# Attention and a two-layer MLP in one kernel: three split products of the second layer in the slots that close a pair, and the second batch's first and last pair summed on VectorE

## The chip, the core and the metric

The kernel runs on one core of one Trainium2 chip. A core has five engines that run side by side and wait for each other through semaphores: TensorE (PE) multiplies matrices, with its weight loads (PEld) shown apart; VectorE (DVE) and ScalarE (ACT) work on elements; GpSimd (POOL) does slower elementwise work and issues some of the DMAs; SyncE (SP) issues the other DMAs. TensorE writes to PSUM, which is divided into banks; everything else lies in SBUF. The metric is device time in microseconds (us), the median of several runs.

## The reference

The inputs are q, k and v of shape 8 x 12 x 448 x 64 (batch, heads, sequence, head size), two gains of 64 numbers, and two matrices of weights, 768 x 2048 and 2048 x 768. All are f32. What is computed, cut to what matters:

```
q_n = q / sqrt(mean(q*q, -1) + 1e-6) * g_q          # the same for k with g_k
scores = q_n @ k_n.T / 8                             # per batch and head, 448 x 448
attn = exp(scores - max) ; attn = attn / (attn.sum(-1) + 1e-9)
x = (attn @ v), heads side by side                   # 3584 x 768
h = x @ w_in ;  g = 0.5*h*(1 + tanh(0.79788*(h + 0.044715*h**3)))
out = g @ w_out                                      # 3584 x 768
```

## The kernel before

**Stages.** The batches b = 0 to 7 are taken in turn. For each there is an attention stage and a stage of the first MLP layer. The second MLP layer of one batch is spread into the attention stage of the next, so that TensorE has work while ScalarE computes exps. So from b = 1 on, `attention(b, ...)` mixes the attention of batch b with a quota of second-layer products of the batches before: 96 for b = 1 and 112 for the others. After it, `mm1(b, f)` computes the first layer of batch b in 16 groups of six matmuls, ended by a GELU on ScalarE. The change's title counts from one: its "batch 2" is b = 1 in the code and in this text.

**Pairs and slots.** The 12 heads of a batch are six pairs, hp = 0 to 5. The keys of a head are cut into four tiles of 112. `scores` (line 198) makes the scores of one key tile for both heads of a pair, two matmuls of 64 rows that run at the same time, into one of two PSUM buffers, and an exp on ScalarE turns them into the bf16 tile `ex`. `attention` (line 359) goes through a pair in two slots. In the even slot it issues the scores of key tiles 0 and 1; in the odd slot those of tiles 2 and 3. An even slot from the second pair on also ends the pair before it (`pair_ends`, line 260): the products of `ex` with v (called x here) into one PSUM tile, and the sums over keys, as products with a matrix of ones, into another. Both write 64 columns per head, so that the two heads' matmuls run at the same time.

**Second-layer products.** They are a list, taken from the front by `upto` (line 365). One output tile takes 16 of them; then VectorE copies the tile to SBUF (line 317), and SP sends out the row when both halves are there. The tiles share two PSUM buffers with the first layer's. In the first pair's two slots 20 and 10 products are issued; after that `even` products in each even slot, ahead of `pair_ends`, each cut into two halves of 64 columns (`parts` = 2), and whole ones in each odd slot, so many that the quota less 30 and less `last` is used up in equal steps. `last` holds how many come before and after the last pair's `pair_ends`.

**Sums over keys.** For b of 2 and more, `key_sums` (line 212) adds the exps of key tiles 0 and 1, and of 2 and 3, on VectorE (line 220); for the first and the last pair it also adds the two results (line 222). The sums then take two steps of two matmuls in the middle pairs, and one step in the first and last pair, in place of four. For b = 1 all pairs take four steps, directly from the exps.

**What VectorE does for a pair.** `pair_recips` transposes the sums (line 244), takes reciprocals (line 245) and transposes back (line 246); `pair_x` multiplies x by them (line 251). VectorE works through its instructions in the order in which they are written out, and the copies of output tiles, the adds of `key_sums`, the gains of the keys (`gain`, line 191, in `side`) and the sums of squares (line 127) stand in the same queue.

**Order.** `manual_schedule` keeps each engine's instructions in the order of the code. `side` and `m1` are plans that say in which slot or first-layer group a preparing step of a later batch is issued. In `m1`, at group 0, GpSimd starts the norms of the next batch (`normed_all`); for b of 2 and more a one-element copy (`gpsimd_waits`, line 527) stands ahead of them that waits for the last pair's added exps. SP issues the transposing DMAs of these norms at groups 4, 8 and 12.

Of the kernel before, what the change touches and what calls it, by code (L numbers as in the profile page):

```python
# [16 lines left out]
def kernel(  # L17
# [19 lines left out]
    HP = H // 2  # L37
# [86 lines left out]
    def total(b, c, n, hs=slice(0, CH)):  # L124
        if b not in sss:
            sss[b] = smp.tile([P, NCH, 2, CH, NK], F32, tag="ss", name="ss")
        nc.vector.reduce_sum(  # L127
            sss[b][:, c, "qk".index(n), hs], sqs[n, b, c][:, hs], axis=AX.X
        )
# [11 lines left out]
    def idle(n, w):  # L141

        for _ in range(n):
            nc.tensor.matmul(w, zeros[:, :128], zeros, start=True, stop=True)
# [51 lines left out]
    exs, ess, oas = {}, {}, {}  # L196

    def scores(b, hp, kt):
        if kt == 0:
            exs[b, hp] = exq.tile([P, NK, 2, S], BF16, tag="ex", name="ex")  # L200
        sc = ps_s.tile([128, 2, 512], F32, tag="sc", name="sc")
        for a in range(2):
            r = slice(a * D, (a + 1) * D)
            nc.tensor.matmul(  # L204
                sc[:, a, :S], kT[r, hp, kt], qT[b][r, hp],
                start=True, stop=True,
            )
        nc.scalar.activation(  # L208
            exs[b, hp][:, kt], sc[:P, :, :S], AF.Exp, scale=scale, bias=shift
        )  # L210

    def key_sums(b, hp, i):


        if b < 2:
            return
        if i == 0:
            ess[b, hp] = exq.tile([P, 2, 2, S], BF16, tag="es", name="es")
        ex, es = exs[b, hp], ess[b, hp]
        nc.vector.tensor_add(es[:, i], ex[:, 2 * i], ex[:, 2 * i + 1])  # L220
        if i == 1 and hp in (0, HP - 1):
            nc.vector.tensor_add(es[:, 0], es[:, 0], es[:, 1])  # L222

    def pair_products(b, hp, what, waits=0):


        o = oas[what] = ps_o.tile([128, S], F32, tag=f"o{what}", name=f"o{what}")
        idle(waits, o)

        e = exs[b, hp] if what or b < 2 else ess[b, hp]  # L230
        n = 1 if not what and b > 1 and hp in (0, HP - 1) else e.shape[1]
        for i in range(n):
            for a in range(2):
                nc.tensor.matmul(  # L234
                    o[a * D:(a + 1) * D], vb[b % 2][:, 2 * hp + a, i] if what else ones, e[:, i, a],
                    start=(i == 0), stop=(i == n - 1),
                )

    def pair_recips():

        st = stp.tile([128, S // 32, 32], F32, tag="st", name="st")
        oas["rb"] = stp.tile([128, S], F32, tag="rb", name="rb")
        rc = smp.tile([128, S // 32], F32, tag="rc", name="rc")
        nc.vector.transpose(st.rearrange("p a b -> p (a b)"), oas[0])  # L244
        nc.vector.reciprocal(rc, st[:, :, 0])
        nc.vector.transpose(oas["rb"], rc.to_broadcast([128, S // 32, 32]))  # L246

    def pair_x(b, hp):
        if hp == 0:
            xT[b] = xp.tile([128, HP, S], BF16, tag="xT", name="xT")  # L250
        nc.vector.tensor_mul(xT[b][:, hp], oas[1], oas["rb"])  # L251
# [7 lines left out]

    def pair_ends(b, hp):  # L260

        for what in (1, 0) if b > 1 else (0, 1):
            pair_products(b, hp, what)
        pair_recips()
        pair_x(b, hp)
# [93 lines left out]
    def attention(b, m2, quota, side):  # L359


        first, last, even = (20, 30), (12, 12) if b > 1 else (17, 7), 2 if b > 1 else 0
        given = 0

        def upto(k, parts=1):
            nonlocal given
            while given < k:
                m2.pop(0)(parts)
                given += 1

        spread = quota - first[1] - sum(last)
        for hp in range(HP):
            for odd in range(2):
                i = 2 * hp + odd
                for fn in side.get(i, ()):
                    fn()
                if hp and not odd:
                    key_sums(b, hp - 1, 1)
                for kt in range(2 * odd, 2 * odd + 2):
                    scores(b, hp, kt)  # L380
                if not hp:
                    upto(first[odd])
                elif odd:
                    upto(first[1] + spread * hp // (HP - 1))
                else:

                    upto(given + even, 2)
                    pair_ends(b, hp - 1)
                if not odd:
                    key_sums(b, hp, 0)  # L390
        key_sums(b, HP - 1, 1)
        nc.scalar.preload_act_table_set(GELU_SET)
        upto(given + last[0])
        pair_ends(b, HP - 1)
        upto(quota)

# [130 lines left out]
    def gpsimd_waits(x):  # L527

        nc.gpsimd.tensor_copy(mark, x)  # L529
# [44 lines left out]
    for b in range(B):  # L574
        m1, side = [], []
        if b == 0:

            m1 = [(1, lambda: total(1, 0, "k"), lambda: total(1, 1, "q"),
                   lambda: total(1, 1, "k"), lambda: total(1, 2, "k"), lambda: total(1, 2, "q"),
                   lambda: nc.scalar.preload_act_table_set(EXP_SET), lambda: rsqrt(1),  # L580
                   lambda: nc.scalar.preload_act_table_set(GELU_SET),  # L581
                   lambda: load_v(1, CH, 2 * CH), lambda: normed1(0), lambda: normed1(1)),
                  (3, lambda: loads(2, 0)),
                  (4, lambda: trans(1, 0, ps_m), lambda: normed1(2), lambda: transposed(1, 1),
                   lambda: loads(2, 1)),
                  (5, lambda: trans(1, 1, ps_m), lambda: loads(2, 2),
                   lambda: pool_waits(1, 2, "k", 1), lambda: square(2, 0, "q", nc.gpsimd),
                   lambda: square(2, 0, "k", nc.gpsimd)),
                  (6, lambda: trans(1, 4, ps_m)), (7, lambda: trans(1, 5, ps_m))]
            side += [(0, lambda: total(2, 0, "q"), lambda: total(2, 0, "k")),  # L590
                     (2, lambda: gain(1, 1))]

            for c, slots in ((1, (5, 7)), (2, (9, 10))):
                for n, slot in zip("qk", slots):
                    side += [(2 * c - 1, lambda c=c, n=n: square(2, c, n, nc.gpsimd)),
                             (slot, lambda c=c, n=n: total(2, c, n))]
        elif b + 1 < B:
            if b > 1:

                m1.append((0, lambda: gpsimd_waits(ess[b, HP - 1][:1, 0, 0, :1])))  # L600
            for c in range(NCH):
                m1 += [(0, lambda c=c: normed_all(b + 1, c)),
                       (4 * c + 4, lambda c=c: transposed(b + 1, c))]
            m1 += [(9, lambda: gain(b + 1, 0)), (14, lambda: gain(b + 1, 1))]
            side.append((3, lambda: gain(b + 1, 2)))
        if 0 < b and b + 2 < B:
            m1 += [(4, lambda: loads(b + 2, 1)), (8, lambda: loads(b + 2, 2))]
            for c, at in ((0, 1), (1, 9)):
                for i, (n, half) in enumerate((n, half) for n in "qk" for half in range(2)):
                    m1.append((at + i, lambda c=c, n=n, half=half: squared(b + 2, c, n, half)))  # L610
                m1 += [(at + 2, lambda c=c: total(b + 2, c, "q")),
                       (at + 4, lambda c=c: total(b + 2, c, "k"))]
            for n in "qk":
                m1.append((13, lambda n=n: square(b + 2, 2, n, nc.gpsimd)))
                side.append((0, lambda n=n: total(b + 2, 2, n)))
        m1 = plan(*m1)
        for f in range(nf // 2 if b == 0 else nf):
            if b > 0:
                mm1(b, f)
            elif f > 1:  # L620
                mm1_pair(f)
            for fn in m1.get(f, ()):
                fn()
        m2 += m2_parts(b)
        if b + 1 == B:
            for fn in m2:
                fn()
            break
        nc.scalar.preload_act_table_set(EXP_SET)
        if b + 2 < B:  # L630
            side += [(11, lambda: rsqrt(b + 2)),
                     (0 if b else 2, lambda: load_v(b + 2, 0, H))]
            if b + 3 < B:
                side.append((1, lambda: loads(b + 3, 0)))
        attention(b + 1, m2, 96 if b == 0 else 112, plan(*side))


# [28 lines left out]
```

## Time and profile before

| | us |
|---|---|
| median of 3 runs (lowest, highest) | 442.35 (442.12, 442.97) |
| the profiled execution's own time | 442.38 |
| its span, first to last instruction | 440.6 |
| attention stage of b = 1 with 96 products (59.60 to 92.06) | 32.46 |
| attention stage of b = 2 with 112 products (110.32 to 142.98) | 32.66 |
| attention stages of b = 3 to 7, each | 32.66 |
| TensorE busy in the stage of b = 2 | 32.54 |
| ScalarE / VectorE busy in the stage of b = 2 | 26.38 / 25.36 |
| first layer of one batch, 96 matmuls | 18.16 |

The granted TensorE clock is 0.999 of full speed over the span. The profile's busy shares count a matmul from its start to its modelled end, so a TensorE that is busy all the time may still wait. What it waits for is seen in the starts of single instructions: a matmul of 448 columns follows its neighbour after 0.19 us when nothing holds it, one of 384 columns after 0.16 us. In lines of the timeline the first number is the start, the second the time from the first start to the last end of a run of equal instructions, and the bracket at the end tells how long the engine was idle before it and what released it.

### The profile page before, as it was taken

Reading aid. Unit: us, or ns where it says so; the run is one execution under the profiler, and the core shown is the slowest. Engines: PE = TensorE matmul, PEld = TensorE weight load, DVE = VectorE, ACT = ScalarE, POOL = GpSimd, SP = SyncE. Lnnn points to the kernel's source line nnn. Section 1 sums busy time; section 2 is a strip of 40 time slices with the busy share of each in tenths; the row PEclk is TensorE's granted clock in tenths of the full one; section 3 lists DMA queues with packets and bytes.
Section 4 is the critical chain, followed back from the end, with each engine's and each line's share of the span. In section 5 each row is a group of like instructions: output and inputs, shape, how many; then the busy total and the mean of one; then the engine's idle time right before and its main releaser. Section 6 shows DMA issues by size and latency. Waiting matters only on the chain.

```text
span 440.6 us, 7132 instructions
## 1 busy us (share of the span) xinstructions
PE 428.7 (97%) x2827; PEld 215.2 (49%) x2827; DVE 258.9 (59%) x446; ACT 306.2 (69%) x407; POOL 149.9 (34%) x138
## 2 busy tenths in 40 slices
PE   8898999999999999999999999999999999999996
PEld 3344554455445554455445544455544554455563
DVE  5889846834688357763688536872588603881010
ACT  5896568946886688857888578856889348863310
POOL 5998126482202940065400950037400730000000
PEclk9999999999999999999999999999999999999999
DMA  8999999569801868139911779119831431111022
GB/s 202 241 233 238 211 190 259 80 152 250 169 18 55 190 111 176 36 93 224 194 37 36 170 159 182 37 37 230 128 70 36 99 65 37 38 36 37 0 72 72
DMA packets 79218, 54.02 MB, mean 123 GB/s; under 512 B 37456, under 2 KB 74192, under 8 KB 79184
## 3 DMA queue, kind: packets, MB, share of 16 engines
q1 hardware_dynamic: 62240, 41.66, 40.5%
q0 software_dynamic: 16624, 11.80, 18.2%
q8 instruction: 22, 0.36, 0.3%
q10 hardware_dynamic: 320, 0.10, 0.1%
q14 instruction: 12, 0.10, 0.1%
HBM read 45.61 MB, written 11.01 MB: 129 GB/s over the span
## 4 chain that ended last, share of the span: by engine, by line
PE 87%; ACT 8%; DMA 3%; DVE 1%; issue 0%; SPq 0%; POOL 0%; ACTq 0%; DVEq 0%
PE o L293 34%; PE h L272 29%; PE o L234 11%; PE sc L204 10%; ACT ex L208 6%; PE hh L339 3%; DMA vb<-in_v_dram 2%; DMA rawq<-in_q_dram 1%; ACT g L344 1%; PE tp L166 0%; SPq L95 0%; ACT L581 0%; ACT L580 0%; POOL g L122 0%; DVE st L244 0%
## 5 line engine op out<-in xcount | busy, mean ns | idle before, releaser
L208 ACT ACTIVATE ex<-sc,shift 112x896 bf16<-112x896 f32 x192 | 182.4, 1003 | 21.6 <-PE sc L204 21.2
L293 PE MATMUL o<-wout,g 128*128 128x384 bf16 (+1 forms) x956 | 161.2, 328 | 0.0
L272 PE MATMUL h<-xT,win 128*128 128x448 bf16 x672 | 128.3, 352 | 0.0
L293 PEld LDWEIGHTS <-g 128*128 128x128 bf16 (+1 forms) x956 | 81.4, 99 | 70.3 <-issue 23.4
L276 ACT ACTIVATE g<-h 128x448 bf16<-128x448 f32 x112 | 61.0, 544 | 75.2 <-PE h L272 72.3
L272 PEld LDWEIGHTS <-win 128*128 128x128 bf16 x672 | 65.8, 98 | 61.0
L127 DVE TENSOR_REDUCE ss<-sq 112x16 f32<-112x1024 f32 (+1 forms) x44 | 50.1, 1143 | 62.1 <-ACT sq L120 58.9
L204 PE MATMUL sc<-qT,kT 64*128 64x448 bf16 x384 | 58.8, 355 | 4.9 <-ACT ex L208 2.7
L317 DVE COPY osb<-o 128x384 f32<-128x384 f32 x51 | 28.1, 551 | 50.9 <-PE o L293 50.0
L220 DVE TENSOR_TENSOR es<-ex 112x896 bf16<-112x896 bf16 x72 | 43.9, 617 | 10.2 <-ACT ex L208 10.0
L529 POOL COPY mark<-es 1x1 bf16<-1x1 bf16 x5 | 0.9, 178 | 140.0 <-DVE es L222 140.0
L244 DVE STREAM_TRANSPOSE st<-o 128x448 f32<-128x448 f32 x48 | 31.2, 649 | 26.7 <-PE o L234 26.0
L234 PE MATMUL o<-ex,vb 112*64 112x448 bf16 x384 | 44.7, 354 | 0.6 <-DMA vb<-in_v_dram 0.6
L149 POOL TENSOR_TENSOR nrmk<-rawk,rinv 112x512 bf16<-112x512 f32 x40 | 44.5, 1130 | 0.0
L149 POOL TENSOR_TENSOR nrmq<-rawq,rinv 112x512 bf16<-112x512 f32 x40 | 41.0, 1043 | 4.8 <-ACT rinv L139 4.8
L204 PEld LDWEIGHTS <-kT 64*128 64x128 bf16 x384 | 17.2, 93 | 46.4 <-issue 41.2
L251 DVE TENSOR_TENSOR xT<-o,rb 128x448 bf16<-128x448 f32 x48 | 30.0, 625 | 3.8 <-PE o L234 1.7
L246 DVE STREAM_TRANSPOSE rb<-rc 128x448 f32<-128x448 f32 x48 | 31.0, 645 | 1.6
L122 POOL TENSOR_TENSOR sq<-rawq 112x1024 f32<-112x1024 f32 x9 | 17.1, 1894 | 40.1 <-DMA rawq<-in_q_dram 26.0
L234 PEld LDWEIGHTS <-vb 112*64 112x64 bf16 x384 | 20.9, 109 | 14.7 <-issue 2.3
L122 POOL TENSOR_TENSOR sq<-rawk 112x1024 f32<-112x1024 f32 (+1 forms) x11 | 19.5, 1774 | 4.9 <-DVE ss L127 3.3
L339 PE MATMUL hh<-xT,win 128*128 128x448 bf16 x96 | 19.1, 352 | 1.4 <-ACT g L344 0.8
(60 smaller groups left out, 235.9 us busy)
## 6 DMA issues: line engine op xcount, KB each, us to landing
rawq<-in_q_dram SPq DMA_DIRECT2D x22, 448.0 KB, 5.4
rawk<-in_k_dram SPq DMA_DIRECT2D x22, 448.0 KB, 6.5
vb<-in_v_dram POOLq DMA_DIRECT2D x6, 672.0 KB, 7.4
win<-in_moe_w_in_dram POOLq DMA_DIRECT2D x2, 1536.0 KB, 18.5
wout<-in_moe_w_out_dram POOLq DMA_DIRECT2D x2, 1536.0 KB, 21.6
out_dram<-osb SPq DMA_DIRECT2D x7, 336.0 KB, 2.7
out_dram<-osb SPq DMA_DIRECT2D x8, 288.0 KB, 2.7
out_dram<-osb SPq DMA_DIRECT2D x8, 240.0 KB, 2.7
```

The lines of the kernel that those rows point to most:

```text
L122: eng.tensor_mul(sq, raw, raw)
L127: nc.vector.reduce_sum(sss[b][:, c, "qk".index(n), hs], sqs[n, b, c][:, hs], axis=AX.X)
L149: eng.tensor_mul(nrms[n, b, c][:, j].rearrange("p t a d -> p a t d"), raws[n, b, c][:, 2 * j:2 * j + 2], rinvs[b][:, c, "qk".index(n), 2 * ...
L204: nc.tensor.matmul(sc[:, a, :S], kT[r, hp, kt], qT[b][r, hp], start=True, stop=True,)
L208: nc.scalar.activation(exs[b, hp][:, kt], sc[:P, :, :S], AF.Exp, scale=scale, bias=shift)
L220: nc.vector.tensor_add(es[:, i], ex[:, 2 * i], ex[:, 2 * i + 1])
L234: nc.tensor.matmul(o[a * D:(a + 1) * D], vb[b % 2][:, 2 * hp + a, i] if what else ones, e[:, i, a], start=(i == 0), stop=(i == n - 1),)
L244: nc.vector.transpose(st.rearrange("p a b -> p (a b)"), oas[0])
L272: nc.tensor.matmul(h[:, :S], win[:, c, f * 128:(f + 1) * 128], xT[b][:, c], start=(c == 0), stop=(c == HP - 1),)
L276: nc.scalar.activation(g[:, f, (b % 2) * S:(b % 2 + 1) * S], h[:, :S], AF.Gelu_apprx_tanh)
L293: nc.tensor.matmul(o[j * m:(j + 1) * m, :HD], g[:, f, i * 128 + j * m:i * 128 + (j + 1) * m], wout[:, f, half * HD:(half + 1) * HD], start ...
L339: nc.tensor.matmul(h[:, j, :S], win[:, c, f * 128:(f + 1) * 128], xT[0][:, c], start=(c == 0), stop=(c == HP - 1),)
```

## The change

- In `attention`, `even` becomes 3 instead of 2 for b of 2 and more. It stays 0 for b = 1. The quota stays, so each odd slot issues one whole product fewer.
- For b = 1, `last` becomes (12, 12) instead of (17, 7), as for the later batches.
- `key_sums` adds exps for the first and last pair of b = 1 too: three adds each on VectorE. The sums of these two pairs then take one step instead of four.
- In `pair_ends` of b = 1, x's products come ahead of the sums for all pairs, as for the later batches.
- In b = 1's first-layer stage GpSimd too waits for the last pair's added exps before the next batch's norms.

```diff
     def key_sums(b, hp, i):
-        if b < 2:
+        if b < 1 or b == 1 and 0 < hp < HP - 1:
             return
...
     def pair_products(b, hp, what, waits=0):
...
-        e = exs[b, hp] if what or b < 2 else ess[b, hp]
-        n = 1 if not what and b > 1 and hp in (0, HP - 1) else e.shape[1]
+        e = exs[b, hp] if what or (b, hp) not in ess else ess[b, hp]
+        n = 1 if not what and b and hp in (0, HP - 1) else e.shape[1]
...
     def pair_ends(b, hp):
-        for what in (1, 0) if b > 1 else (0, 1):
+        for what in (1, 0):
             pair_products(b, hp, what)
...
     def attention(b, m2, quota, side):
-        first, last, even = (20, 30), (12, 12) if b > 1 else (17, 7), 2 if b > 1 else 0
+        first, last, even = (20, 30), (12, 12), 3 if b > 1 else 0
...
         elif b + 1 < B:
-            if b > 1:
-                m1.append((0, lambda: gpsimd_waits(ess[b, HP - 1][:1, 0, 0, :1])))
+            m1.append((0, lambda: gpsimd_waits(ess[b, HP - 1][:1, 0, 0, :1])))
```

## The prediction

> **What bounds the kernel now.** I read the page's busy shares and its chain first, for which engine holds the end and which waits get into the chain; then the timeline of one steady stretch of attention, engine by engine, for what a slot waits on; then VectorE's timeline near the end of an attention stage, and that of the second batch. Times are microseconds.
>
> ```profile
> PE 428.7 (97%) x2827; PEld 215.2 (49%) x2827; DVE 258.9 (59%) x446; ACT 306.2 (69%) x407; POOL 149.9 (34%) x138
> ...
> PE 87%; ACT 8%; DMA 3%; DVE 1%; issue 0%; SPq 0%; POOL 0%; ACTq 0%; DVEq 0%
> ```
>
> TensorE is the chain, but 8% of it is ScalarE: exps that TensorE waited for. Where, the timeline of batch b = 4 shows. TensorE:
>
> ```profile
> 222.44 0.55 PE L204 MATMUL sc<-qT,kT 64*128 64x448 bf16 x4
> 222.92 0.52 PE L293 MATMUL o<-wout,g 128*64 128x384 bf16 x4
> 223.27 0.93 PE L234 MATMUL o<-ex,vb 112*64 112x448 bf16 x8
> 224.03 0.54 PE L234 MATMUL o<-es,ones 112*64 112x448 bf16 x4
> 224.51 0.66 PE L204 MATMUL sc<-qT,kT 64*128 64x448 bf16 x4
> 225.10 1.80 PE L293 MATMUL o<-wout,g 128*128 128x384 bf16 x10
> 226.83 0.55 PE L204 MATMUL sc<-qT,kT 64*128 64x448 bf16 x4
> ```
>
> ScalarE, and TensorE's weight loads, over the same stretch:
>
> ```profile
> 222.85 1.91 ACT L208 ACTIVATE ex<-sc,shift 112x896 bf16<-112x896 f32 x2 [0.44 <-PE sc L204]
> 224.91 1.91 ACT L208 ACTIVATE ex<-sc,shift 112x896 bf16<-112x896 f32 x2 [0.16 <-PE sc L204]
> ```
>
> ```profile
> 224.50 0.11 PEld L204 LDWEIGHTS <-kT 64*128 64x128 bf16 x3 [0.36 <-issue]
> 224.81 0.09 PEld L204 LDWEIGHTS <-kT 64*128 64x128 bf16 x1 [0.19 <-issue]
> ```
>
> An even slot (222.44 to 224.51) has two score tiles, two second-layer products cut in halves, then the pair's x and sums; an odd slot has two score tiles and 9 or 10 whole products. The scores have two buffers, so a slot's second score tile needs the last exp of the slot before. That gives one number for all that follows. A slot's scores start at S; its exps start at S + 0.41 (222.85), take 1.91, and the tile that they free is written 0.05 later (224.76 to 224.81): the next slot's second score tile can't start before **S + 2.36**. Left alone it starts 0.20 after the first. So a slot shorter than 2.16 makes TensorE wait at the next: the even slot above lasts 2.07, and its successor waited 0.09 (224.71 wanted, 224.81 got). The odd slot lasts 2.32 and nobody waited.
>
> VectorE where the last pair's stage ends (b = 2):
>
> ```profile
> 135.79 0.65 DVE L244 STREAM_TRANSPOSE st<-o 128x448 f32<-128x448 f32 x1 [1.02 <-PE o L234]
> ...
> 138.51 0.55 DVE L317 COPY osb<-o 128x384 f32<-128x384 f32 x1
> ```
>
> The pair's sums (their last matmul starts at 135.40) release a chain of 0.39 + 2.71 before VectorE reaches the copy of a finished output tile, which ends at 139.06. TensorE needs that tile's buffer for product 96 of the stage's 112, the nineteenth of the run below, at 136.27 + 0.17 + 17 x 0.1625 = 139.21: a margin of 0.1.
>
> ```profile
> 136.27 3.75 PE L293 MATMUL o<-wout,g 128*128 128x384 bf16 x22
> ```
>
> And b = 1, VectorE:
>
> ```profile
> 65.45 0.45 DVE L194 TENSOR_SCALAR kT<-kT,gcol 128x896 bf16<-128x896 bf16 x1 [2.48 <-DMA kT<-nrmk]
> 66.64 0.65 DVE L244 STREAM_TRANSPOSE st<-o 128x448 f32<-128x448 f32 x1 [0.74 <-PE o L234]
> ```
>
> The gain of the keys waits for a transposing DMA, and stands in VectorE's queue ahead of what the change adds there.
>
> **Three products instead of two in the even slots, b = 2 to 7.** The quota per stage stays, so the odd slots lose one each: 9, 10, 9, 10, 10 become 8, 9, 8, 9, 9. Total work is the same but for 30 more weight loads. A split product takes 0.16 (222.924 to 223.111 to 223.274, starts of single instructions), a whole one 0.1625. Output tiles still end in the same slots (products 31, 47, 63, 79, 95, 111), so VectorE's copies and SP's output DMAs keep their place in each queue.
>
> Now the recursion, from the second score tile T of an even slot to the next such T, with 2.36 as above. Even slot: 0.28 to the products, 0.35 (two) or 0.51 (three), x 0.76, sums 0.19, 0.285 to the next scores: 1.87 or 2.03 to 2.04. Odd slot from its T: 0.29 + 0.17 + 0.1625 (n - 2) + 0.26: 2.03, 1.87 and 1.70 for 10, 9 and 8 (the terms rounded, so a hundredth is lost).
> Before, the even slot is the short one: T' is tied to S + 2.36, then comes the odd work, and T to T is 4.39 with 10 and 4.23 with 9, as the trace has it.
> After, the even slot is 2.24 and its wait is gone; but the odd slot is 0.20 + 1.87 = 2.07 or 1.90, under 2.16, and the wait is there instead, 0.11 with 9 and 0.27 with 8. T to T is 2.04 + 2.36 = **4.40 with either**.
> Along one batch, after minus before: into pair 2's slot -0.03 (the first even slot has a single step of sums and waited 0.28, so the third product fits in; less its one product in the odd slot); into pair 3's +0.01; into pair 4's +0.17 (4.40 for 4.23); into pair 5's +0.01. From there to the last pair's x: the even wait of 0.09 goes, so -0.10; and the tile copy comes in. It is tied to the pair's sums: 0.39 + 2.71 + 0.55 + 0.05 = 3.71 after them. TensorE now reaches product 96 at 0.285 + 0.20 + 0.28 + 0.17 + 16 x 0.1625 = 3.54, one product and a wait sooner than before (3.81). It waits 0.17. Sum: -0.03 + 0.01 + 0.17 + 0.01 - 0.10 + 0.17, **+0.24 a batch** with the digits dropped here, six batches +1.45. Ends: +0.07 a batch if the copy is not waited for, +0.36 if the third split product costs 0.187, as the first does.
> The last pair's x is covered (its exps end some 1.6 before it), and its sums need VectorE's adds 4.9 after the sums before and come at 5.24.
>
> One rule speaks against this part. The row first: the second split product's two weight loads start at 222.951, while the first product's matmuls (222.924) run on the same rows, and nothing is lost. The Trainium skill, "TensorE: Matmul & The Clock Gate", Part 3 (packing small matmuls), says that a weight load overlaps running matmuls only where its row group differs. By that rule each third product would pay its load too, which is the last rival below; by the row it doesn't, and I go by the row.
>
> **The second batch (b = 1).** Six adds on VectorE (0.62 each, as L220 and L222 have them), twelve matmuls fewer, which run two at a time: six steps of 0.188.
> Pair 0: x now goes first and ends its steps where sums could start at 66.43. But the adds queue behind the gain: 65.45 + 0.36, first add 0.65, second 0.63, 0.05 to TensorE: 67.14. Its successor scores start at 67.43 instead of 67.29: **+0.14**, and it stays, since the next slot's limit is tied to them by 2.36. Without the wait it would be -0.21.
> Pairs 1 to 4: x before sums. The reciprocals' chain starts 0.78 later and frees x's bank 0.23 before the next x needs it: nothing. V of heads 4 to 11 lands at 74.29, and x of pair 2 will want it at 74.37, where sums used to go first: nothing, at most 0.6.
> Last pair: three steps fewer, -0.57. But VectorE is late: the squares' two sums (82.6 to 84.85 after the shift), the chain, and the new add bring the copy of the tile that ends with product 63 to 87.55 instead of 86.27; its buffer is free at 88.15, and product 80 is reached at 87.86: +0.30. The final adds end at 89.30, before the sums at 89.68, which costs nothing. Products of 12 and 12 cover the chain of reciprocals as 7 and the x did: it ends at 92.35, and the first layer needs it at 92.87. The exps of the last pair shift 0.67 behind the later squares' sums on ScalarE, and are still done 1.4 before x.
> GpSimd's new wait holds its twelve norms (1.0 each) from 85.09 to 89.5. Behind them on SP stand the transposing DMAs, the first issued after the fifth first-layer group, at 97.6; its four norms end at 93.5. Nothing; without that cover, up to 4.4.
> Sum for b = 1: +0.14 - 0.57 + 0.30, **-0.14** with the digits (ends -0.8 without either wait, +0.7 with late V).
>
> Together +1.45 - 0.14 = +1.3 on the profiled execution's 442.38 (span 440.6 and 1.8 around it; the median of the runs is 442.35, so no correction): **443.7**.
>
> **Rivals.** *The copy is not waited for* (VectorE's chain a tenth or two shorter, or TensorE later at product 96): 6 x 0.07 - 0.14 = +0.3, 442.6, no change. For it: I work with margins of 0.17 there. Against it: the chain repeats to 0.01 in all six stages. If it is b = 1 that goes without its two waits, +1.45 - 0.8 gives 443.0, no change either.
> *The odd slots have room*: their next scores don't wait for exps, TensorE runs through, and only the filled even waits count: -0.44 a batch, 439.6, faster. It decides at an odd slot of 2.16, which is ten products; with 8 and 9 it needs exps that start a tenth to a quarter sooner than 0.41 after the scores. Against it: every slot below 2.16 in this trace waits by the difference, b = 1's odd slots of eight too (0.21 at 69.24 and 0.27 at 73.48).
> *Weights of the third split product are exposed*: 30 x 0.109 (the mean of that load) = +3.3 more, 447.0. Against it: the loads at 222.951.
>
> **How the numbers follow.** Forecast 0.69, with a range of its own of 443.2 to 444.4; no change by the missing copy wait or by b = 1, 0.20; odd slots with room 0.07; exposed weights 0.04. About 0.03 of the forecast falls within 0.2%, which is some 0.9 here and about what a measurement can tell. So faster 0.07, within 0.2% 0.23, slower 0.70. The range leaves out the faster rival and the exposed weights and takes in the others: 442.4 to 444.6.
>
> **What would show it.** Right: even slots without the 0.09 wait, every odd slot's successor with a T 0.3 to 0.5 after S, T to T 4.40 in all of pairs 2 to 5; a gap of 0.17 in the last run of whole products in six stages; stages of b = 2 to 7 longer by 0.24 each; in b = 1, sums of pair 0 at 67.1 and a gap near 87.9. Wrong: T to T below 4.3 after slots of eight (the limit of 2.36 isn't one), or no gap at product 96.

## The result

The changed kernel takes 443.94 (median of 7 runs, 443.01 to 444.86) where the kernel before takes 442.30 (7 runs, 441.82 to 442.97). The ratio is 1.0035, with a 95% interval of 1.0022 to 1.0049: slower by a third of a percent, against a forecast of 443.7.

The profiled execution took 444.00, with a span of 442.2. It is set against the one of before, 442.38 with 440.6. The changed kernel's profile begins with these busy shares, and has this chain of work that ended last:

```profile
PE 429.2 (97%) x2845; PEld 213.1 (48%) x2845; DVE 263.5 (60%) x452; ACT 306.4 (69%) x407; POOL 150.3 (34%) x139
...
PE 82%; DMA 7%; ACT 6%; DVE 3%; issue 2%; SPq 0%; POOL 0%; ACTq 0%; DVEq 0%
```

TensorE is still busy 97% of the time by this count. In the chain VectorE and DMA have grown (1% and 3% before, 3% and 7% now).

Stage by stage, from the start of a stage's first whole product to the start of its first layer, by the starts of single instructions (the 32.66 in the table ahead of the prediction is counted from the first scores, 0.48 earlier):

| | before | changed | difference |
|---|---|---|---|
| b = 1 | 32.465 | 32.255 | -0.21 |
| b = 2 | 32.179 | 32.437 | +0.26 |
| b = 3 to 7, each | 32.179 | 32.432 to 32.433 | +0.25 |
| from a first layer's start to the next stage | 18.74 | 18.74 | 0 |

The sum is +1.32. Of the 1.6 between the two spans, another 0.27 lies ahead of the stage of b = 1 (it starts at 59.60 and 59.87), where the two programs are the same. This start moves from one profile to the next: it lies between 58.79 and 60.00 in the ten profiled kernels that have the same instructions ahead of it. So the stages show what the change does, and the time of the whole program adds an offset that moves without it.

The wait is now one slot further on. TensorE in the odd slot of pair 3 and the even slot of pair 4 of b = 2, from the changed kernel's timeline:

```profile
127.29 0.55 PE L204 MATMUL sc<-qT,kT 64*128 64x448 bf16 x4
127.77 1.47 PE L293 MATMUL o<-wout,g 128*128 128x384 bf16 x8
129.18 0.84 PE L204 MATMUL sc<-qT,kT 64*128 64x448 bf16 x4
129.94 0.68 PE L293 MATMUL o<-wout,g 128*64 128x384 bf16 x6
130.46 0.93 PE L234 MATMUL o<-ex,vb 112*64 112x448 bf16 x8
131.22 0.55 PE L234 MATMUL o<-es,ones 112*64 112x448 bf16 x4
131.69 0.55 PE L204 MATMUL sc<-qT,kT 64*128 64x448 bf16 x4
```

The weight loads of the scores at 129.18, and ScalarE over the same stretch:

```profile
129.17 0.11 PEld L204 LDWEIGHTS <-kT 64*128 64x128 bf16 x3 [0.32 <-issue]
129.65 0.09 PEld L204 LDWEIGHTS <-kT 64*128 64x128 bf16 x1 [0.37 <-issue]
```

```profile
127.69 3.80 ACT L208 ACTIVATE ex<-sc,shift 112x896 bf16<-112x896 f32 x4 [0.45 <-PE sc L204]
```

The odd slot from 127.29 now has eight products and lasts 1.89. The scores behind it take 0.84 instead of 0.55: the second tile's load stands at 129.65, 2.36 after the odd slot's scores, where the exps have freed the buffer. Four exps run without a break. The even slot from 129.18 ends in scores of 0.55, without the wait that it had before.

The last pair of the same stage, TensorE and then VectorE:

```profile
136.58 3.75 PE L293 MATMUL o<-wout,g 128*128 128x384 bf16 x21
```

```profile
136.21 0.65 DVE L244 STREAM_TRANSPOSE st<-o 128x448 f32<-128x448 f32 x1 [1.07 <-PE o L234]
...
138.92 0.55 DVE L317 COPY osb<-o 128x384 f32<-128x384 f32 x1
```

21 products take as long as 22 did: between the 17th and the 18th of the run, which is product 96, lie 0.335 instead of 0.1625. Product 96 starts 0.05 after the copy's end at 139.47.

### The profile page after: what moved, and what is told of

The parts are those of the page before. It is cut to its first block, busy times and chain, and to the rows that moved or that the text cites. A ratio compares the mean times of both kernels' runs of the same rounds, so it can differ in the third digit from the quotient of the medians.

```text
span 442.2 us, 7170 instructions
## 1 busy us (share of the span) xinstructions
PE 429.2 (97%) x2845; PEld 213.1 (48%) x2845; DVE 263.5 (60%) x452; ACT 306.4 (69%) x407; POOL 150.3 (34%) x139
## 4 chain that ended last, share of the span: by engine, by line
PE 82%; DMA 7%; ACT 6%; DVE 3%; issue 2%; SPq 0%; POOL 0%; ACTq 0%; DVEq 0%
PE o L293 31%; PE h L272 29%; PE o L234 11%; PE sc L204 9%; ACT ex L208 4%; DMA kT<-nrmk 3%; DMA vb<-in_v_dram 2%; PE hh L339 1%; DMA rawq<-in_q_dram 1%; DVE ss L127 1%; DVE rb L246 0%; DVE st L244 0%; DVE xT L251 0%; ACT g L344 0%; SPq L95 0%
## 5 line engine op out<-in xcount | busy, mean ns | idle before, releaser
L220 DVE TENSOR_TENSOR es<-ex 112x896 bf16<-112x896 bf16 x76 | 46.4, 617 | 9.5 <-ACT ex L208 9.3
L204 PEld LDWEIGHTS <-kT 64*128 64x128 bf16 x384 | 16.1, 93 | 47.6 <-issue 44.0
L234 PEld LDWEIGHTS <-vb 112*64 112x64 bf16 x384 | 20.3, 109 | 15.5 <-issue 3.7
```

What stands on the lines that cost most here:

```text
L204: nc.tensor.matmul(sc[:, a, :S], kT[r, hp, kt], qT[b][r, hp], start=True, stop=True,)
L234: nc.tensor.matmul(o[a * D:(a + 1) * D], vb[b % 2][:, 2 * hp + a, i] if what else ones, e[:, i, a], start=(i == 0), stop=(i == n - 1),)
```

## The experiments

My theory: a slot's scores tie the next slot's second score tile to 2.36 after them, and VectorE's copy of an output tile ties product 96 to the sums before; these two make the loss in b = 2 to 7. The rivals: the third split product is dear in itself (its weight loads, its halves); or the loss comes from the second batch's part, from its adds, its order or GpSimd's wait. The runs, with the stages measured as above (the single times that the expectation on the gain names are 0.23 less than in the changed kernel's timeline, a rough shift to the timeline of the kernel before, whose stage of b = 1 starts 0.27 earlier):

| | time, median | ratio to before (95%) | stage b = 1 | stage b = 2 to 7 |
|---|---|---|---|---|
| second batch's part alone | 442.91 | 1.0009 (0.9991 to 1.0027) | 32.56 | 32.18 |
| three products alone | 443.91 | 1.0029 (1.0015 to 1.0044) | 32.47 | 32.43 |
| three and ten | 440.01 | 0.9938 (0.9924 to 0.9953) | 32.55 | 31.63 |
| three whole products | 446.88 | 1.0100 (1.0077 to 1.0123) | 32.12 | 32.95 |
| first add behind the copy | 442.08 | 0.9996 (0.9974 to 1.0018) | 32.15 | 32.26 |
| sums first in middle pairs of b = 1 | 442.98 | 1.0010 (0.9986 to 1.0034) | 32.07 | 32.42 |
| gain behind the adds | 443.19 | 1.0020 (0.9996 to 1.0045) | 33.12 | 32.43 |
| two and ten | 441.97 | 0.9992 (0.9968 to 1.0017) | 32.56 | 32.18 |
| gain behind the adds, V earlier | 443.06 | 1.0017 (1.0003 to 1.0030) | 31.97 | 32.43 |
| all together | 437.73 | 0.9892 (0.9868 to 0.9917) | 31.39 | 31.63 |

Measured beside these runs, the kernel before had medians of 442.05 to 442.31. A stage of b = 2 to 7 repeats to about 0.01 from batch to batch and between kernels that have the same instructions in it. So a difference of 0.1 in these stages is read from a profile, while the times of one kernel's runs lie 0.6 to 4.9 apart. The stage of b = 1 doesn't repeat so well, as the first run shows.

### The second batch's part alone

```diff
-        first, last, even = (20, 30), (12, 12), 3 if b > 1 else 0
+        first, last, even = (20, 30), (12, 12), 2 if b > 1 else 0
```

> The second batch's part alone (even slots of b = 2 to 7 back at two products). By the theory of the limit of 2.36 the later stages come back to 32.18 from the first whole product to the first layer, as before, and the stage of b = 1 keeps the -0.21 that the changed kernel's profile shows: 442.1, so 0.2 below before. By the rival that the added adds, the turned order and GpSimd's wait cost something behind the stage of b = 1 (late norms, late transposes), the first layer after it or a later stage grows and the time is above before.

The later stages are at 32.179 as before, and the time between them is 18.74: the wait on GpSimd and the later norms cost nothing. The stage of b = 1, though, is 32.56 here and 32.26 in the changed kernel, with the same instructions in it. The difference is pair 0. VectorE and TensorE, this kernel:

```profile
65.44 0.45 DVE L194 TENSOR_SCALAR kT<-kT,gcol 128x896 bf16<-128x896 bf16 x1 [2.14 <-DMA kT<-nrmk]
```

```profile
67.13 0.38 PE L234 MATMUL o<-es,ones 112*64 112x448 bf16 x2 [0.74 <-DVE es L222]
```

The changed kernel's profile:

```profile
65.61 0.45 DVE L194 TENSOR_SCALAR kT<-kT,gcol 128x896 bf16<-128x896 bf16 x1 [1.84 <-DMA kT<-nrmk]
```

```profile
67.31 0.38 PE L234 MATMUL o<-es,ones 112*64 112x448 bf16 x2 [0.45 <-DVE es L222]
```

The brackets tell the idle time: here TensorE is idle 0.29 longer ahead of these sums. The transposing DMA landed 6.02 after the stage's first whole product here, and 5.72 after it in the changed kernel. Two more profiles have the same instructions up to the first layer of b = 1: with three whole products it landed at 5.58 and the stage is 32.12; with two and ten, at 6.02 and 32.56. A landing later by 0.30 makes the stage longer by 0.30. So the part changes the stage of b = 1 by anything from -0.35 to +0.1, from one profiled execution to another, and the time of this run can't be told from before. Of the 0.8 between 442.91 and the 442.1 that I had expected, this explains 0.3; the 12 runs lie between 441.62 and 446.50, and what moved the others I don't know.

### The three products alone

```diff
-        first, last, even = (20, 30), (12, 12) if b > 1 else (17, 7), 2 if b > 1 else 0
+        first, last, even = (20, 30), (12, 12) if b > 1 else (17, 7), 3 if b > 1 else 0
```

(This one is against the kernel before.)

> The three products alone (b = 1 as before). Theory: +0.25 in each of six stages, 443.8, and the stage of b = 1 is 32.47 as before. Rival: if part of the loss comes from b = 1's part, less than +1.5.

443.91, and each of six stages +0.25. The stage of b = 1 is 32.465 as before. The whole loss is here, and the second batch's part is no part of it.

### Three products and ten

```diff
-        first, last, even = (20, 30), (12, 12), 3 if b > 1 else 0
+        first, last, even = (20, 30), (7, 10) if b > 1 else (6, 10), 3 if b > 1 else 0
```

> The changed kernel with ten products in every odd slot, taken from the last run of the stage: last is (7, 10) for b of 2 and more, (6, 10) for b = 1, in place of (12, 12). The work is the same. Theory: both slots of a pair are then longer than 2.16, so no second score tile waits for exps except in the slot after the first pair (0.12); T to T is 4.47 with 13 products where it was 4.40 with 11 or 12; the copy of the tile that ends with product 79 is no longer in the last pair's chain. A stage of b = 2 to 7 is 0.7 to 0.8 shorter than the changed kernel's 32.43, that of b = 1 about 0.9 shorter than 32.26: 438.7. By the rival that the third split product is what costs (its weights, its halving), the stages keep the changed kernel's length or nearly, 443 to 444.

440.01: 3.9 below the changed kernel and 2.3 below the one before, with the same three split products. The slots of a middle pair, TensorE and ScalarE:

```profile
125.45 0.55 PE L204 MATMUL sc<-qT,kT 64*128 64x448 bf16 x4
125.93 0.68 PE L293 MATMUL o<-wout,g 128*64 128x384 bf16 x6
126.44 0.93 PE L234 MATMUL o<-ex,vb 112*64 112x448 bf16 x8
127.20 0.55 PE L234 MATMUL o<-es,ones 112*64 112x448 bf16 x4
127.68 0.55 PE L204 MATMUL sc<-qT,kT 64*128 64x448 bf16 x4
```

```profile
125.86 1.91 ACT L208 ACTIVATE ex<-sc,shift 112x896 bf16<-112x896 f32 x2 [0.31 <-PE sc L204]
128.09 1.91 ACT L208 ACTIVATE ex<-sc,shift 112x896 bf16<-112x896 f32 x2 [0.32 <-PE sc L204]
```

From pair 2 on all scores take 0.55, and ScalarE waits 0.31 ahead of each slot's exps: the even slots last 2.23 and the odd ones 2.22, above the 2.16. A stage is 0.80 shorter than the changed kernel's. The rival of the dear third product falls with it.

I had expected 438.7, and two things are missing. The first layer's second group of matmuls waits 0.12 in each stage: with only ten products behind the last pair, the copy of the last output tile comes too late for its buffer (18.86 from first layer to next stage, 18.74 elsewhere). And b = 1 isn't 0.9 shorter but 0.29 longer:

```profile
88.49 0.95 PE L234 MATMUL o<-ex,vb 112*64 112x448 bf16 x8
90.23 0.38 PE L234 MATMUL o<-es,ones 112*64 112x448 bf16 x2 [0.80 <-DVE es L222]
```

```profile
89.55 0.62 DVE L222 TENSOR_TENSOR es<-es 112x896 bf16<-112x896 bf16 x1
```

With 16 products ahead of the last pair in place of 21, the sums are due at 89.27 and the added exps are ready at 90.2. VectorE's queue, not the exps, is what those products cover there. Part of the 0.29 isn't this wait: the transposing DMA landed at 5.88 after the stage's start, 0.16 later than in the changed kernel's profile, and the sums of pair 0 came 0.15 later.

### Three whole products

```diff
-                    upto(given + even, 2)
+                    upto(given + even)
```

> The changed kernel with the even slots' three products whole instead of cut in halves. Theory: the cut costs nothing and saves the change of shape ahead of x, about 0.1 in each of five slots; a stage grows by 0.5 to 33.0 and the time to 447.0. Rival (halves expose their weight loads): whole products are faster, up to 3 below the changed kernel.

446.88, and 32.95 a stage, +0.52 on the changed kernel. The even slot of pair 3 in b = 2 behind its scores (products, then x and sums of pair 2), TensorE:

```profile
124.95 0.66 PE L293 MATMUL o<-wout,g 128*128 128x384 bf16 x3
125.55 0.95 PE L234 MATMUL o<-ex,vb 112*64 112x448 bf16 x8
126.33 0.54 PE L234 MATMUL o<-es,ones 112*64 112x448 bf16 x4
```

From the first product to the sums there are 1.37, and 1.27 with halved ones (129.945 to 131.215 in the changed kernel): 0.1 in each of five slots. The second and third halved product cost 0.163 from start to start, like whole ones.

### The first add behind the copy

```diff
-                if not odd:
+                if odd == (hp == HP - 1):
                     key_sums(b, hp, 0)
```

> The changed kernel with one edit: the last pair's first add of exps stands behind the odd slot's products in VectorE's queue, so behind the copy of the output tile, not ahead of it. Theory: the copy comes 0.53 earlier and nobody waits for its buffer: product 96 of b = 2 to 7 goes 0.17 earlier, product 80 of b = 1 goes 0.30 earlier, -1.3 in all, 442.6. If the copy is not what TensorE waits for there, the gaps of 0.33 and 0.46 stay and the time with them.

VectorE and TensorE at the last pair of b = 2:

```profile
137.21 0.55 DVE L317 COPY osb<-o 128x384 f32<-128x384 f32 x1
137.67 1.15 DVE L220 TENSOR_TENSOR es<-ex 112x896 bf16<-112x896 bf16 x2
```

```profile
135.40 3.59 PE L293 MATMUL o<-wout,g 128*128 128x384 bf16 x21
```

The run of 21 takes 3.59 instead of 3.75, its gap is gone, and each stage is shorter by 0.176. In b = 1 the gap of 0.46 at product 80 is gone as well; the transposing DMA landed later in this profile (5.91 after the stage's start), so that its stage gains 0.10 only. What is left of the loss in a stage is 32.26 - 32.18 = 0.08, the slots' share, for which the prediction has 0.07 ("if the copy is not waited for"). So one instruction's place in VectorE's queue makes up for two thirds of the loss in these stages. 442.08 is 0.5 lower than the 442.6 that I had expected; in the profile the stage of b = 1 starts at 58.79, 1.07 earlier than in the changed kernel's.

### Sums first in the middle pairs of b = 1

```diff
-        for what in (1, 0):
+        for what in (0, 1) if b == 1 and 0 < hp < HP - 1 else (1, 0):
             pair_products(b, hp, what)
```

> The changed kernel with the sums ahead of x again in the four middle pairs of b = 1. Theory: VectorE's chain of pair 4 starts 0.76 earlier and with it the copy of the tile that ends with product 63, so the gap of 0.46 at product 80 goes to 0.16 and the stage of b = 1 from 32.26 to 31.95; nothing else moves, 443.6. If instead the new add of exps alone makes that copy late, the gap stays.

The run of products ahead of the last pair's x in b = 1, first the changed kernel's and then this one's:

```profile
85.28 3.88 PE L293 MATMUL o<-wout,g 128*128 128x384 bf16 x21
```

```profile
84.44 3.59 PE L293 MATMUL o<-wout,g 128*128 128x384 bf16 x21
```

The gap at product 80 is a usual step again, 0.30 less. The stage is 32.07 and not 31.95, because pair 0's sums waited 0.10 longer on the DMA in this profile. So the turned order in pair 4 makes that copy late. The run with the first add moved shows that the add does too: the copy is late by both, and taking away either is enough.

### The gain behind the adds

```diff
+                ahead = b == 1 and i == 2
+                if ahead:
+                    key_sums(b, hp - 1, 1)
                 for fn in side.get(i, ()):
                     fn()
-                if hp and not odd:
+                if hp and not odd and not ahead:
                     key_sums(b, hp - 1, 1)
```

> The changed kernel with the gain of the keys behind the two adds of the first pair in b = 1. Theory: the adds start when their exps are done (65.3) and not when the transposing DMA has landed; sums of pair 0 start near 66.65 instead of 67.08, and the stage of b = 1 is 0.28 shorter, 31.97. If TensorE waits for the exps there anyway, the stage keeps its length.

```profile
66.41 0.38 PE L234 MATMUL o<-es,ones 112*64 112x448 bf16 x2
66.72 0.36 PE L204 MATMUL sc<-qT,kT 64*128 64x448 bf16 x2
67.31 0.36 PE L204 MATMUL sc<-qT,kT 64*128 64x448 bf16 x2 [0.22 <-ACT ex L208]
...
74.94 0.95 PE L234 MATMUL o<-ex,vb 112*64 112x448 bf16 x8 [1.09 <-DMA vb<-in_v_dram]
```

The wait of pair 0's sums shrank from 0.61 to 0.20, as expected, and then x of pair 2 waited for its V: this kernel's stage is 0.87 longer than the changed one's. It was due at 73.78, 0.29 after its second score tile, and came 1.16 later. In the kernel before, the sums stood ahead of this x and covered 0.78 of such a delay.

### The gain behind the adds, and V of two heads earlier

```diff
-             lambda: w_out_part(0), lambda: load_v(1, 0, CH), lambda: w_out_part(1))]
+             lambda: w_out_part(0), lambda: load_v(1, 0, 6), lambda: w_out_part(1))]
...
-                   lambda: load_v(1, CH, 2 * CH), lambda: normed1(0), lambda: normed1(1)),
+                   lambda: load_v(1, 6, 6), lambda: normed1(0), lambda: normed1(1)),
```

(Beside the edit of the run before.)

> The kernel with the gain behind the first pair's adds, and V of heads 4 and 5 of b = 1 loaded with heads 0 to 3, ahead of the second half of the second layer's weights, not behind them. In the run with the gain moved, x of pair 2 waited 1.16 for that V (landed at 74.76). Theory: the wait goes, pair 2's products follow their scores after 0.29, and the stage of b = 1 is 0.28 shorter than the changed kernel's 32.26: 31.97. If the stage is no shorter, the earlier sums of pair 0 were worth nothing and TensorE waits for exps there.

31.965: the wait for V is gone, and the earlier sums are worth the 0.28 to 0.29 that the recursion gave them. The program's time, 443.06, is 0.9 below the changed kernel's, more than 0.3 explains. In the profiles most of the rest lies ahead of the stage of b = 1, which starts at 59.23 here and at 59.87 in the changed kernel; by the starts named above that need not come from the edit.

### Two products and ten

```diff
-        first, last, even = (20, 30), (12, 12), 3 if b > 1 else 0
+        first, last, even = (20, 30), (10, 12) if b > 1 else (12, 12), 2 if b > 1 else 0
```

> Two products in the even slots of b = 2 to 7 and ten in every odd slot: last is (10, 12). The control for three and ten. Theory: the even slot is 2.07 and its successor waits 0.09 in every pair, T to T is 4.39; what the odd slots get is taken from the last run at the same price, so a stage is 32.18 as before, and the time that of the second batch's part alone, 442.1. If a shorter last run is what helps, this kernel is faster too, by about 0.3 for two products.

441.97, and a stage of 32.176, where the kernel before has 32.179. The scores that open the even slot of pair 3 in b = 2, and those that open its odd slot:

```profile
124.66 0.55 PE L204 MATMUL sc<-qT,kT 64*128 64x448 bf16 x4
...
126.73 0.66 PE L204 MATMUL sc<-qT,kT 64*128 64x448 bf16 x4
```

The even slot lasts 2.07, and the scores behind it wait 0.09 as in the kernel before. Ten in the odd slots alone gain nothing, three in the even slots alone lose; the two together gain 0.55 a stage on the kernel before and 0.80 on the changed one.

### All together

```diff
-        for what in (1, 0):
+        for what in (0, 1) if b == 1 and 0 < hp < HP - 1 else (1, 0):
             pair_products(b, hp, what)
...
-        elif b + 1 == B and half == 0:
+        elif b + 1 == B and half == 0 or osbs.get("act"):
             nc.scalar.copy(part, o[:, :HD])
...
-        first, last, even = (20, 30), (12, 12), 3 if b > 1 else 0
+        first, last, even = (20, 30), (7, 10) if b > 1 else (9, 12), 3 if b > 1 else 0
...
         pair_ends(b, HP - 1)
+        osbs["act"] = True
         upto(quota)
+        osbs["act"] = False
```

(With the gain behind the adds and V of two heads earlier, as above.)

> What the runs so far point to, together: ten products in the odd slots beside three in the even ones for b of 2 and more, last = (7, 10); nine in b = 1, last = (9, 12); the stage's last output tile copied on ScalarE, so that the first layer's second group doesn't wait 0.12 for its buffer; in b = 1 the gain behind the adds, sums ahead of x in the middle pairs, and V of heads 4 and 5 loaded earlier. The work is the same. Theory: stages of b = 2 to 7 as in the run with ten products, 31.63, with the first layer back at 18.74 from group to scores; b = 1 at 31.3: 437.5. If the copy on ScalarE or the order in b = 1 costs elsewhere, 439 to 440.

437.73, 1.1% below the kernel before. The last output tile's copy is on ScalarE, which has nothing else to do there; the first 20 matmuls of the first layer run without a gap:

```profile
142.09 0.48 ACT L315 COPY osb<-o 128x384 f32<-128x384 f32 x1 [2.55 <-PE o L293]
143.23 0.54 ACT L276 ACTIVATE g<-h 128x448 bf16<-128x448 f32 x1 [0.66 <-PE h L272]
```

```profile
141.90 3.95 PE L272 MATMUL h<-xT,win 128*128 128x448 bf16 x20
```

The first layer is back at 18.74, the later stages at 31.63, and b = 1 at 31.39.

## Why the prediction was right

443.7 was forecast, 443.94 measured. The stages give +1.32 where +1.3 was forecast, and +1.64 lies between the two medians; in the profiles the other 0.3 lies ahead of these stages, where the programs are the same, and that it was no more is luck.

- **The limit of 2.36 after a slot's scores.** Shown. From pair 2 on the scores behind even slots lost their wait, and those behind odd slots got it: the second score tile comes 0.31 after the first with nine products and 0.47 with eight, where it was said to be 0.2 + 0.11 and 0.2 + 0.27. (The slot lengths that the prediction prints beside this, 2.07 and 1.90, would give 0.09 and 0.26; the slots lasted 2.05 and 1.89.) From T to T the middle pairs of b = 2 are 4.406 to 4.407; the recursion said 4.40 with either number. That three and ten together run freely, and either alone doesn't, is the limit's own test.
- **The copy at product 96.** Shown: a gap of 0.335, a wait of 0.17 as worked out, which goes when the copy comes earlier.
- **+0.24 a batch.** 0.25 to 0.26, and term by term: -0.02, +0.02, +0.18 and +0.02 into pairs 2 to 5, +0.07 from there to the first layer, where the prediction has -0.03, +0.01, +0.17, +0.01 and -0.10 + 0.17.
- **The split product costs what a whole one does.** Shown by the row that I went by (the starts of the six halves, one step of 0.19 and one of 0.16) and by the run with whole ones, which was slower by the 0.5 of the change of shape. The Trainium skill, "TensorE: Matmul & The Clock Gate", Part 3, has weight loads overlap running matmuls only in another row group, in its list of what overlaps; its account of the mechanism in the same part also allows loads into a background weight buffer. Halves in the same rows overlapped here: in the changed kernel the second product's loads start at 129.972, while the first one's matmuls run from 129.945.
- **b = 1: -0.14.** -0.21 in the profile of the changed kernel. Last pair: the gap at product 80 is 0.46, a wait of 0.30 as worked out. Pair 0: the sums came at 67.04 on the scale of the prediction (67.31 less the 0.27 between the starts), not 67.14, but this rests on when a DMA lands, and among profiles of the same instructions the stage is anywhere between 32.12 and 32.56. I had one landing and took it for a constant. That the result is within 0.1 of the forecast is luck.
- **Order of x and sums: nothing, at most 0.6.** Nothing in the changed kernel's profile. The bound was too low: in the run with the gain moved, the V that x now needs first landed 1.16 late. Some 0.3 of that is the earlier x of that kernel; in the changed one, where x of pair 2 starts 14.71 after the stage's start, the latest landing seen (15.53) would cost 0.8, by my estimate. The step had one landing, like the one above, and not how far it moves from one execution to the next.
- **GpSimd's wait: nothing.** Shown by the unchanged time behind the stage.

## What to carry to other kernels

Two buffers between a producer and a consumer set a shortest useful slot: here a slot below 2.16 makes TensorE wait for the difference in the next one, whatever work stands in it. Before a product is moved from one slot to another, compare both slots with that length: filling a short slot from one that is then too short moves the wait, and work should come from a place that has more than it must cover (the run at a stage's end). Then look where a queue in program order, VectorE's here, has a copy that someone needs behind work that nobody waits for yet.

## What was not expected

- The landing of one transposing DMA in the same stretch of instructions was 5.58, 5.72, 6.02 and again 6.02 after the stage's start in four profiles, and the stage followed it one for one. The V of heads 4 to 11 landed between 11.7 and 15.5 after the stage's start in the ten profiles in which its load was whole. The stage of b = 1 as it was before stood in two profiles (the kernel before and the three products alone) and took 32.465 in both: there the sums of pair 0 don't go through VectorE, and sums stand ahead of x. The DMA landed at 5.82 in one and 6.13 in the other, so that stage didn't follow it.
- With these two out of the way and the products shifted, the six runs of the last kernel lie between 437.51 and 438.58. That isn't less scatter: the six runs of three and ten, which has both, lie between 439.76 and 440.35.
- The kernel before had 0.55 a stage to give in these slots; the change took its three products from the one place that had nothing to spare.
